# Cosformer attention and a token mixer in one kernel: another order of the same steps, with 16 half products of v on GpSimd and eps of four groups by TensorE

## The chip, the cores and the metric

The kernel runs on one core of a Trainium2 chip. A core has TensorE (matmuls and transposes, which write to PSUM), VectorE (DVE), ScalarE (ACT), GpSimd (POOL) and SyncE (SP), which here issues all DMAs between HBM and SBUF. The metric is the time of one execution on the device in microseconds, as the median of several runs.

## The reference

Attention with a linear kernel over 8 batches, 8 heads, 576 positions and head size 64, then a token mixer over the result. With c = cos and s = sin of pi/2 * position / 576:

```python
def phi(x, c, s):
    r = np.maximum(x, 0.0)
    return np.concatenate([r * c, r * s], axis=-1)
kv = einsum('bhsf,bhsd->bhfd', phi(k), v)
num = einsum('bhsf,bhfd->bhsd', phi(q), kv)
den = einsum('bhsf,bhf->bhs', phi(q), phi(k).sum(axis=2)) + 1e-06
x = (num / den), heads side by side: [8, 576, 512]
W = (x @ w_q) @ (x @ w_k).T / sqrt(64)        # [8, 576, 576]
out = relu(W @ x) @ w_out
```

## The kernel before

The work is cut into 16 groups H of four heads (two pairs of heads), two for each batch b = H // 2. The kernel has one function for each kind of step, and a string, `ORDER` (lines 26 to 67), names every step in the order in which it is issued; the loop at line 555 reads it word by word. Each engine works through its own steps in that order and waits, by semaphores, for what a step needs. So the order of the string is, for each engine, the order of its queue: a step that waits holds all later steps of its engine.

A word is a kind, a number, `a` or `b` where it is half a step (one of the two pairs of heads), `:n` for the PSUM bank where a TensorE step writes (eight banks; most steps take a pair of them, MX, KV, QT, N, XT and XR; WK, WQ, KX and WO take one), and `@A`, `@V`, `@G` for the engine where it can be chosen: ScalarE, VectorE, GpSimd.

- Loads by SP: LK, LQ, LV bring k, q, v of one group in halves of 288 KB into `raw` (line 117), five buffers each, so that a load of group H waits until group H - 5 has been read. LW brings the weights. ST stores a block of 128 output rows from one of 16 `o` buffers.
- RK and RQ (lines 222 and 225) are the relus of k and q to bf16, on any of three engines. The product of v with cos and sin is made in one of two ways: VG (line 239) on GpSimd straight from the loaded v, or CV (line 229), a cast to bf16 on any engine, and then VS (line 232) on VectorE.
- KV (line 268) makes the sums over positions on TensorE, KE (line 304) takes them to SBUF. QT (line 290) transposes q, QM (line 312) multiplies it with cos and sin on VectorE; groups in `QT_WIDE` have another shape of these.
- N (line 332) makes numerator and denominator of half a group, g = 2H or 2H + 1. EP (line 354) adds eps to the denominator; groups in `EPS_PE` have it added by two small matmuls (line 348) instead. RC (line 377) takes the reciprocal of one g, RJ (line 380) of both of a group, X (line 383) multiplies: x in SBUF. RC, RJ and X are VectorE's.
- XT or XR transposes x on TensorE, XE evicts it. WK and WQ are the products of x with w_k and w_q, KW and QW evict them. KX is the product of x with WK's result, [64, 512]; XK evicts it and XA and XB copy halves across partitions. MX makes the mixed rows of a quarter of a batch, ME evicts them with the relu. WO (line 504) multiplies 128 rows with w_out: its rows i count over two batches, nine blocks to each pair; OE evicts, ST stores.
- WU are warm-up matmuls; T steps make tables.

The product with w_k comes first for keys, so the 576 x 576 matrix is never made. v2, rk, rq, vb, qm, kv, x, xT have two buffers each: KV of group H must be through before VG or VS of group H + 2 begins, and so on. In PSUM a step waits until the last reader of its banks is done: `KV0:2` then `N1:2` means that N1 waits for KE0. No step is planned at run time; the string is the whole schedule.

Lines of the profile name the helper: L205 is the relu on VectorE or GpSimd, L203 on ScalarE, L209, L211 and L213 are casts and copies on ScalarE, GpSimd and VectorE, whichever step asked for them; the tile names tell which it was.

Of the kernel before, what the change touches and what calls it, by code (L numbers as in the profile page):

```python
# [43 lines left out]
WO8:1 ME10@V ME11@A RK8a@G LQ11b ME9@A VS9 QT9:6 OE8:5@A LQ10b KV8:4 OE3:6@A LK10b WU4:1 RK9a@G QM9
KE8@A XR7:2 MX8:0 N16:4 VG10a LK11b ME8@A KV9:6 XE7@V EP16@A LK11a RQ11a@A WO10:0 RC16 KE9@A LK12a
X16 WK3:1 LK10a VG10b OE10:7@V N17:4 KW3@A N19:6 LV11b EP17@V N18:0 RC17 EP19@A X17 KX3:2 LQ13b
WQ3:3 EP18@V RJ9 XK3@A LV12b RQ11b@A WO12:4 XA3@G QW3@V LV12a XB3@A VG11a X18 RQ10@A WO11:5 X19
WO2:0 OE12:8@A LQ15b RK11b@A LQ12a QT11:6 OE2:9@V OE11:10@A RK11a@G LK13b XT9:2 RK10b@A LQ14b QM11
XT8:0 XE9@A VG11b LQ14a WO5:5 XE8@V LQ12b RK10a@A QT10:6 MX15:0 MX12:2 QM10 WK4:4 ME12@A CV12@G
# [5 lines left out]
KW5@A ST16 KV13:2 QM13 LV15b VG14b MX16:6 LV15a KE13@A KX5:4 ME16@A LK15a MX17:0 N26:2 XK5@V LK15b
ME17@A N24:6 EP26@V N25:4 RC26 RK14@A X26 WO18:0 XB5@G RQ15@G EP24@V EP25@A RC24 WO20:1 X24
OE18:12@A XA5@G RC25 N27:2 X25 OE20:6@A WQ5:0 ST20 EP27@V RC27 KV14:4 QW5@A X27 VG15 MX20:0 XR12:6
KE14@V ME20@A XR13:2 QT14:4 XE12@A XE13@V WO21:0 QM14 RK15b@A WO15:1 RK15a@A OE21:15@V QT15:4 MX22:6
N28:2 QM15 ME22@A ST21 WK6:0 EP28@A ST11 OE15:6@A KV15:6 ST6 RC28 KW6@A X28 ST4 N29:4 KE15@A MX23:0
ST2 MX21:6 ME23@V KX6:2 ST10 ME21@A ST17 WQ6:3 EP29@A XK6@A RC29 ST1 N30:6 XA6@G QW6@V N31:0 X29  # L60
XB6@G EP30@A ST13 WO22:3 EP31@A ST18 RC30 X30 WO24:2 OE22:10@A ST7 RC31 X31 WO19:3 ST8 ST0 OE24:9@V
MX26:0 OE19:3@A XR15:6 ST9 XR14:4 XE15@V WO26:3 XE14@A ST15 ME26@V ST22 WO23:2 OE26:1@V WK7:4
OE23:13@A ST26 MX27:0 ST12 MX25:6 KW7@V MX24:2 ME27@A WQ7:5 ME24@V ST23 ME25@A KX7:4 ST19 WO28:6
XK7@A ST24 QW7@A XA7@G WO30:7 XB7@G OE28:11@V MX28:4 ST28 MX29:2 ME28@A WO27:6 ME29@V OE30:10@A
MX31:2 MX30:4 OE27:1@V ST30 ME31@A WO25:7 ME30@A ST27 WO29:6 OE25:13@A WO32:4 ST25 OE29:3@V WO31:7
# [5 lines left out]
def kernel(  # L71
# [240 lines left out]
    def QM(H, ps, eng):  # L312
        if H in QT_WIDE:
            q_t = qt_wide(place["QT", H]).rearrange("p c (r d) -> p r c d", r=2)
            for r in range(2):
                V.tensor_mul(  # L316
                    qm_b[H % NQM][:, :, r, 0:C, :],
                    q_t[:, r].unsqueeze(1).to_broadcast([P, 2, C, H2]), qtab)
# [58 lines left out]
    def RC(g, ps, eng):  # L377
        V.reciprocal(rec(g), num(place["N", g])[:, :, :, D:D + 1] if g in EPS_PE else rec(g))  # L378

# [219 lines left out]
```

## Time and profile before

| | before |
|---|---|
| median of 3 runs | 121.09 us (120.91 to 121.33) |
| the profiled execution | 120.56 us, its span 118.8 us |
| granted TensorE clock | 0.998 |
| busy: TensorE, VectorE, ScalarE, GpSimd | 96.0, 90.9, 83.9, 72.1 us |
| moved | 29.62 MB read, 9.44 MB written |

The span runs from the first to the last instruction that the profiler saw. A row of a timeline or of the chain of waits has the start, the length, the engine and line, and the tiles written and read; a row in square brackets tells how long the engine had been idle and what ended it. A row of the groups has the count, the busy time in all and the mean of one in ns. A suffix q means the engine's sequencer, which waits or issues.

### The profile page before, as it was taken

Reading aid. Unit: us, or ns where it says so; the run is one execution under the profiler, and the core shown is the slowest. Engines: PE = TensorE matmul, PEld = TensorE weight load, DVE = VectorE, ACT = ScalarE, POOL = GpSimd, SP = SyncE. Lnnn points to the kernel's source line nnn. Section 1 sums busy time; section 2 is a strip of 40 time slices with the busy share of each in tenths; the row PEclk is TensorE's granted clock in tenths of the full one; section 3 lists DMA queues with packets and bytes.
Section 4 is the critical chain, followed back from the end, with each engine's and each line's share of the span. In section 5 each row is a group of like instructions: output and inputs, shape, how many; then the busy total and the mean of one; then the engine's idle time right before and its main releaser. Section 6 shows DMA issues by size and latency. Waiting matters only on the chain.

```text
span 118.8 us, 4916 instructions
## 1 busy us (share of the span) xinstructions
PE 96.0 (81%) x2068; PEld 66.8 (56%) x2079; DVE 90.9 (76%) x160; ACT 83.9 (71%) x151; POOL 72.1 (61%) x66
## 2 busy tenths in 40 slices
PE   0020797669799789989989989999999999999970
...
DVE  2039699786997998989989787888899988855360
...
GB/s 107 304 370 408 393 388 338 383 390 393 387 393 392 384 389 393 394 389 387 387 391 390 283 348 289 290 345 206 206 279 103 91 302 377 404 393 383 337 299 177
DMA packets 20662, 39.38 MB, mean 332 GB/s; under 512 B 3232, under 2 KB 3232, under 8 KB 20640
## 3 DMA queue, kind: packets, MB, share of 16 engines
...
HBM read 29.62 MB, written 9.44 MB: 329 GB/s over the span
## 4 chain that ended last, share of the span: by engine, by line
PE 48%; DVE 18%; DMA 15%; POOL 5%; issue 5%; ACT 4%; SPq 1%; DVEq 0%; ACTq 0%; POOLq 0%
PE ps L509 19%; DMA vraw<-in_v_dram 10%; DVE qm L316 7%; DVE x L393 5%; DMA kraw<-in_k_dram 5%; PE ps L285 5%; PE ps L340 4%; PE ps L466 4%; PE ps L489 3%; POOL v L248 3%; PE ps L439 3%; PE ps L295 2%; PE ps L452 2%; PE ps L275 2%; PE ps L419 2%
## 5 line engine op out<-in xcount | busy, mean ns | idle before, releaser
L248 POOL TENSOR_TENSOR v<-vraw,vtab 128x1152 bf16<-128x1152 f32 (+1 forms) x16 | 45.1, 2829 | 17.5 <-DVE rec L378 11.4
L509 PE MATMUL ps<-wow,mix 128*128 128x512 bf16 x133 | 33.1, 380 | 0.8 <-issue 0.3
L393 DVE TENSOR_TENSOR x<-ps,rec 128x640 bf16<-128x640 f32 x32 | 25.9, 822 | 1.2
L509 PEld LDWEIGHTS <-mix 128*128 128x128 bf16 x144 | 12.9, 98 | 14.7 <-issue 0.9
L500 ACT ACTIVATE mix<-ps 128x576 bf16<-128x576 f32 x25 | 15.7, 653 | 5.7 <-PE ps L489 5.6
L209 ACT COPY o<-ps 128x512 f32<-128x512 f32 x22 | 12.7, 585 | 9.2 <-PE ps L509 9.0
L316 DVE TENSOR_TENSOR qm<-ps,qtab 128x1152 bf16<-128x1152 bf16 x22 | 15.6, 749 | 0.8 <-PE ps L295 0.8
L211 POOL TENSOR_SCALAR kx<-kx 64x256 bf16<-64x256 bf16 x12 | 6.3, 524 | 14.6 <-ACT kx L209 12.1
L340 PE MATMUL ps<-kvs,qm 64*128 64x65 bf16 x640 | 13.8, 193 | 1.3 <-ACT kvs L209 0.9
L203 ACT ACTIVATE rq<-qraw 128x576 bf16<-128x576 f32 (+1 forms) x15 | 13.1, 880 | 2.1 <-DMA qraw<-in_q_dram 1.9
L340 PEld LDWEIGHTS <-qm 64*128 64x128 bf16 x640 | 12.5, 96 | 3.2 <-issue 2.6
L213 DVE COPY o<-ps 128x512 f32<-128x512 f32 x14 | 9.6, 688 | 5.6 <-PE ps L509 4.7
L203 ACT ACTIVATE rk<-kraw 128x576 bf16<-128x576 f32 (+1 forms) x17 | 12.3, 739 | 0.2
L209 ACT CAST kvs<-ps 128x260 bf16<-128x260 f32 (+1 forms) x14 | 6.6, 471 | 8.1 <-PE ps L275 4.2
L285 PE MATMUL ps<-v,rk 64*64 64x130 bf16 x360 | 7.5, 228 | 5.1 <-DVE v L234 4.0
L209 ACT COPY xT<-ps 128x1152 bf16<-128x1152 bf16 (+1 forms) x8 | 9.3, 1169 | 0.7 <-PE ps L406 0.5
L285 PEld LDWEIGHTS <-rk 64*64 64x64 bf16 x360 | 6.3, 111 | 6.0 <-issue 4.3
L234 DVE TENSOR_TENSOR v<-vb,vtab 128x2304 bf16<-128x2304 bf16 (+1 forms) x8 | 9.1, 1148 | 0.4 <-PE ps L285 0.3
L301 PE MATMUL ps<-ident,rq 64*128 64x64 bf16 x90 | 2.4, 200 | 8.3 <-ACT rq L203 7.3
L489 PE MATMUL ps<-wq,kx 64*128 64x288 bf16 x64 | 8.1, 287 | 0.4 <-DVE x L393 0.4
L275 PE MATMUL ps<-v,rk 64*128 64x260 bf16 x108 | 7.1, 271 | 1.5 <-DVE qm L316 0.9
L295 PE MATMUL ps<-ident,rq 128*128 128x128 bf16 x99 | 7.8, 228 | 0.0
...
## 6 DMA issues: line engine op xcount, KB each, us to landing
...
```

The costliest lines, as they stand in the source:

```text
L203: A.activation(dst, s, AF.Relu)
L209: A.copy(dst, s)
L213: V.tensor_copy(dst, s)
L248: G.tensor_mul(dst[:, part, :, :, 0:D], s[:, part].unsqueeze(3).to_broadcast([P, n, C, 2, D]), vtab.unsqueeze(1).to_broadcast([P, n, C, 2, ...
L285: nc.tensor.matmul(kv_v[o, r, :], rk_of(H)[a, pr, c, :], v2_b[H % NV2][a, pr, c, :, 0:D + 1], start=(c == 0), stop=(c == C - 1))
L295: nc.tensor.transpose(qt_v[:, c, :], rq_b[H % NPREP][:, c, :, :], ident)
L316: V.tensor_mul(qm_b[H % NQM][:, :, r, 0:C, :], q_t[:, r].unsqueeze(1).to_broadcast([P, 2, C, H2]), qtab)
L340: nc.tensor.matmul(nv[:, pr, u, :], qm_b[H % NQM][a, s, r, 2 * u:2 * u + 2, :], kv_b[H % 2][a, r, pr if H in KV_WIDE else 0, s, 0:D + 1], ...
L393: V.tensor_tensor(x_b[b % NX][:, :, 4 * h:4 * h + 4, :].rearrange("p u (w r) d -> p r w u d", r=2)[:, r], nv[:, :, :, 0:D], rec(g).to_broa ...
L489: nc.tensor.matmul(pair(ps)[:, t, :].bitcast(FP32)[:, 0:HS], kx_b[b % 2][a, (m // 2) ^ t, (m % 2) * P:(m % 2 + 1) * P], wq_b[b % 2][a, :], ...
L500: A.activation(dst, s, AF.Relu, scale=scale_moe)
L509: nc.tensor.matmul(o, mix_b[bp % 2][:, m, rt * P:(rt + 1) * P], wow[:, m, :], start=(m == 0), stop=(m == NDM - 1))
```

## The change

`ORDER` is replaced as a whole: 651 words in place of 656. The same functions and buffers are used. Counted over both strings: VG 13 halves and 3 whole groups before, 8 and 4 after (19 and 16 halves); VS 5 whole and 3 halves before, 6 and 4 after. GpSimd takes 5 steps of CV (4 before), 4 of CW (3), 11 of RK (8), 7 of RQ (6), 1 of XB (6). VectorE evicts 8 OE (14), 6 XE (8), 5 KE (2), 8 ME (7); ScalarE 28 OE (22), 10 XE (8), 11 KE (14), 24 ME (25). EP falls from 30 to 28, RC rises from 22 to 24, RJ falls from 5 to 4. Warm-up matmuls are 5 and 1 before, 1 and 2 after. Every TensorE step of the computation is there in both. The engine of a step and its PSUM bank change too. The start and the end of both strings, and the lines around the loads of k for groups 13 and 14:

```diff
@@ ORDER @@
-LV0b TB TQ LQ0b LQ0a TI LV1b TW LK0a LV1a TK LV0a TZ CV0b@A LK0b T2 LV2b LQ1a RQ0@A LQ1b LK1a TV
-QT0:0 RK0a@V LK2b CV1b@V QM0 LK1b CV1a@A LV2a CV0a@A VS1b LQ2a RK0b@A VS0 LQ2b LK2a CV2b@V KV0:0
-VS1a LV3a KE0@A VS2b LV3b RQ1@A N0:0 LW1 N1:2 RK2b@A LQ3b QT1:4 EP1@V RK1a@A RC1 X1 VG2a LQ3a RK1b@A
-WU22:6 QM1 RQ2a@A LW0 KV1:2 LK3a RQ2b@V LK3b RK2a@G KE1@A RC0 QT2:4 X0 LV4b N2:2 KV2:6 QM2 VG3 LQ4a
-N3:0 KE2@A LV4a EP2@V CW1@A N5:6 EP3@A LK4b N4:4 RJ1 EP5@A X2 RQ3@A LQ4b X3 LQ5b XT0:2 CW0@A LQ5a
-EP4@V RK3a@A XT1:0 RC4 X4 LK4a XE0@A RK3b@G QT3:4 LV5b VG4b XE1@A QM3 KV3:2 LV5a LK5a WK0:0 RC5
-KE3@A X5 LK5b N7:2 KW0@A N6:4 RQ4a@G EP7@V RC7 KX0:0 RQ4b@A LV6b X7 VG4a RK4b@A QT4:6 LV6a RC6 X6
-XK0@A XT2:2 RQ5a@A LV7b QM4 WQ0:0 RK4a@A LQ7b XR3:4 RQ5b@G QW0@A KV4:6 LQ7a XE3@A CV5b@V XE2@V
-CV5a@G LQ6b QT5:0 KE4@A XB0@G LK6a WK1:4 VS5 N9:6 LK6b KW1@A MX3:2 RK5b@A N8:4 RK5a@G QM5 LV7a EP9@A
-ME3@A KV5:0 VG6 LQ6a XA0@A EP8@V RJ4 LK7a X9 KX1:2 KE5@A LK7b X8 N10:0 N11:6 RQ7@A LW4 EP10@V XT4:4
-EP11@V RJ5 LW3 X11 WQ1:3 XE4@A LW2 X10 MX2:6 QW1@A MX1:4 LW5 RK6@V XK1@A XR5:0 ME2@A QT7:2 XA1@G
-XE5@V LV8b ME1@A XB1@G KV6:6 CV7@A QM7 RQ6@G LQ8b MX5:4 LQ8a WK2:2 KE6@A VS7 MX0:0 ME5@A LQ9b QT6:6
-KW2@A LK8b MX6:4 RK7b@A KX2:3 QM6 CW3@G LQ9a ME0@A WQ2:2 RK7a@G LV8a ME6@A MX4:0 QW2@V ME4@A CW2@G
-LK8a KV7:6 CW4@V MX7:0 LV9a CW5@G XK2@V KE7@A N13:4 ME7@V XA2@A N14:6 XB2@G LV9b EP13@A N12:2 VG8b
-EP14@A RC13 WO7:0 EP12@V RQ8a@A X13 LK9b RQ8b@A WO1:1 RC12 LQ11a X12 LK9a QT8:4 OE7:0@V OE1:1@A
...
-X23 WO13:2 ST14 RK12@A QM12 RQ13@G WO17:3 LK14a LK14b OE13:13@A XR11:0 XA4@G OE17:14@A XR10:4 RK13@G
...
-ST29 OE32:9@A WO33:6 ST32 OE31:10@V WO35:4 ST31 OE33:1@V WO34:7 ST33 OE35:13@V ST35 OE34:9@A ST34
+LV0a TB TK LQ1a TQ TV LV0b WU6:0 LQ0a LV1a TI LV1b T2 LQ0b TW TZ LK0b LK0a LQ1b CV0@G LV2b LK2b
+CV1a@V LK1a CV1b@V LV2a VS0 RQ0b@A LK1b RK0b@A LQ2b VS1 RK0a@A LQ2a RQ0a@V RQ1@G LK2a QT0:0 LV3b
+KV0:2 QM0 LK3b LV3a QT1:4 KE0@A CV2b@V RK2b@V LQ3b WU10:6 VS2b LW1 N1:2 RK1@G QM1 N0:0 EP1@A LQ3a
+KV1:4 RQ2@A LK3a CV2a@V EP0@V VS2a LV4b RK2a@G QT2:6 RC0 X0 LV4a VG3b QM2 RK3b@A LQ4a KV2:0 KE1@A
+LK4a RC1 N2:4 KE2@A N3:6 RC2 N4:0 X1 VG3a LW0 CW1@A X2 LQ4b XT0:2 RQ3b@A LV5a RC3 N5:4 XE0@A X3 LV5b
+EP4@V RQ3a@G EP5@V XT1:6 RC4 RK3a@A X4 LK4b VG4b QT3:2 XE1@A RC5 LQ5a KV3:0 QM3 LQ5b WK0:6 KE3@V
+LK5b LK5a VG4a X5 N6:0 N7:2 EP6@A LV6a RQ4@A XT2:4 RC6 KW0@V LQ7b X6 EP7@A XE2@A QT4:6 LV6b RC7
+CV5@G X7 KX0:0 LQ6b CW0@A QM4 XR3:2 RK4a@A RK4b@G LK6b WQ0:1 XE3@A KV4:6 LQ6a RQ5@V XK0@A LW4 VS5
+QT5:2 KE4@A WK1:0 LQ7a RK5@A XA0@G QM5 N9:6 N8:4 LW3 KW1@A KV5:2 XB0@A LK6a EP8@A EP9@V RC8 X8 KX1:0
+VG6 LW2 KE5@A QW0@A RC9 N10:2 X9 LQ8a XK1@A N11:4 EP10@A MX3:0 LV7a EP11@V MX2:6 ME3@A RJ5 X10 XB1@A
+LW5 XT4:0 ME2@A X11 LV7b WQ1:2 RQ6@A XE4@V LQ8b MX0:4 XR5:6 RQ7@A QW1@V LQ11b ME0@V MX7:2 CW4@G
+QT6:0 LK7b ME7@A XE5@V QT7:4 XA1@G LK7a RK6@A CW3@G QM6 WK2:6 LV8a CW2@G MX1:0 KW2@A KV6:2 LK8a
+ME1@A QM7 CW5@G LK9b MX5:0 MX6:6 ME5@A WQ2:4 CV7@G LK8b KE6@V KX2:5 QW2@A ME6@V LV8b N13:2 N12:0
+VS7a LV9a MX4:6 WO1:4 ME4@A VS7b LV10b EP13@A EP12@A WO6:6 OE1:0@A RJ6 RK7a@G LQ10b X12 RK7b@A WO4:4
+RQ8@G LV9b OE6:1@A XK2@V X13 KV7:0 LQ9b OE4:2@A XA2@G XB2@A QT8:6 KE7@V LQ9a VG8a XR6:4 QM8 N14:0
...
+ME11@V LK11b RQ9@G MX9:4 KE8@V XR7:0 ME9@A LK10a N17:2 VS9 XE7@A QT9:4 LK13a WO10:6 RK9a@A RQ11a@G
+QM9 WK3:0 OE10:6@A RQ11b@G LK14a KV9:4 LK11a KW3@V VG10 LV12b WQ3:6 RC17 KE9@A X17 CV11a@A LV13a
...
+WO35:1 ST33 OE32:13@V WO34:2 ST32 OE35:8@V ST35 OE34:4@A ST34
@@ sizes @@
-    EPS_PE = (0, 6)
+    EPS_PE = (2, 3, 17, 19)
...
-    QT_WIDE = (1, 4, 5, 6, 7, 8, 9, 10, 11, 12, 14)
+    QT_WIDE = (1, 4, 5, 6, 7, 8, 9, 10, 11, 12, 15)
```

A word such as `WU22:6` means 22 // 4 = 5 warm-up matmuls of shape 2.

More of the change, by code (lines that the diff above doesn't have):

```diff
@@ L44 @@
[L44 to L49, printed above, removed]
@@ L50 @@
-ME15@A KV10:6 OE5:11@V KW4@A KV11:2 KE10@A VS12 ST5 MX13:4 KE11@A N20:6 ME13@A LK12b MX14:0 KX4:2
-LK13a EP20@A VG13a ME14@A WQ4:3 RC20 LV14b X20 XK4@A LV14a N21:0 RQ12a@A N23:4 LQ15a EP21@V QW4@A
-N22:6 RC21 ST3 X21 WO9:2 RQ12b@A VG13b EP23@A EP22@A WO14:3 XB4@A RJ11 OE9:11@A X22 QT12:0 OE14:12@A
-X23 WO13:2 ST14 RK12@A QM12 RQ13@G WO17:3 LK14a LK14b OE13:13@A XR11:0 XA4@G OE17:14@A XR10:4 RK13@G
-XE11@V MX18:6 KV12:2 ME18@A XE10@V RQ14@A MX19:0 VG14a WO16:6 KE12@V ME19@V WK5:7 OE16:6@A QT13:0
@@ L55 @@
[L55 to L65, printed above, removed]
-ST29 OE32:9@A WO33:6 ST32 OE31:10@V WO35:4 ST31 OE33:1@V WO34:7 ST33 OE35:13@V ST35 OE34:9@A ST34
+LV0a TB TK LQ1a TQ TV LV0b WU6:0 LQ0a LV1a TI LV1b T2 LQ0b TW TZ LK0b LK0a LQ1b CV0@G LV2b LK2b
@@ new lines @@
+VS7a LV9a MX4:6 WO1:4 ME4@A VS7b LV10b EP13@A EP12@A WO6:6 OE1:0@A RJ6 RK7a@G LQ10b X12 RK7b@A WO4:4
+RQ8@G LV9b OE6:1@A XK2@V X13 KV7:0 LQ9b OE4:2@A XA2@G XB2@A QT8:6 KE7@V LQ9a VG8a XR6:4 QM8 N14:0
+LK9a XE6@A N15:2 WO7:6 LV11a EP14@V RC14 EP15@A X14 LQ11a WO3:7 VG8b OE7:3@A RK9b@A LK10b MX10:0
+MX8:4 OE3:4@V RK8@A WO8:6 LV10a RC15 X15 WO0:7 LQ10a ME10@A CV9@G ME8@A LV11b MX11:0 KV8:2 OE8:5@A
+ME11@V LK11b RQ9@G MX9:4 KE8@V XR7:0 ME9@A LK10a N17:2 VS9 XE7@A QT9:4 LK13a WO10:6 RK9a@A RQ11a@G
+QM9 WK3:0 OE10:6@A RQ11b@G LK14a KV9:4 LK11a KW3@V VG10 LV12b WQ3:6 RC17 KE9@A X17 CV11a@A LV13a
```

22 lines of the change are left out of this document (20 added, 2 removed).

## The prediction

> **What bounds the kernel now.** I read the page first, then stages of the span, then the chain of waits with the timeline beside it, then the groups of instructions by shape.
>
> ```profile
> span 118.8 us, 4916 instructions
> PE 96.0 (81%) x2068; PEld 66.8 (56%) x2079; DVE 90.9 (76%) x160; ACT 83.9 (71%) x151; POOL 72.1 (61%) x66
> ...
> PE   0020797669799789989989989999999999999970
> ...
> DVE  2039699786997998989989787888899988855360
> ```
>
> TensorE has almost nothing to do for four slices (12 us), is 60 to 90% busy until about slice 16, and is full from there to the end; VectorE is at 80% or more for most of that time. So two things can move the end: how much of TensorE's work is left when it becomes full, and the idle time after that. I cut the span where the opening ends, at the start of KV7, the moment after QM6, the last of the eight QM steps 0 to 7 on VectorE:
>
> ```profile
> 0.00:7.91 7.91, 0.58 (x18) 0.50 (x18) 0.81 (x6) 5.42 (x9) 3.39 (x17) 1.00 0.75 242
> ...
> 0.00:46.35 46.35, 29.68 (x700) 24.15 (x700) 34.09 (x62) 34.37 (x57) 30.02 (x36) 1.00 1.01 362
> 46.35:118.80 72.45, 66.31 (x1370) 42.62 (x1379) 56.78 (x99) 49.50 (x94) 42.08 (x32) 1.00 0.86 312
> ```
>
> The columns are the stage, its length, then busy time of TensorE, its weight loads, VectorE, ScalarE and GpSimd, the granted clock, the DMA share and GB/s. The chain of waits ends on TensorE:
>
> ```profile
> 45.05 0.67 PE ps L466 x10
> 45.72 0.49 PE ps L452 x8
> 46.20 0.23 PE ps L489 x2
> ...
> 108.92 6.16 PE ps L509 x28
> ```
>
> The last product ends at 108.92 + 6.16 = 115.08; the last eviction, store and landing fill the 3.7 us to 118.8. From 46.35 to 115.08 are 68.73 us with 66.31 busy: only 2.42 us of idle TensorE is left to win there. Before 46.35 TensorE was busy 29.68 us, so 16.7 us idle: the opening is where an order can win or lose.
>
> VectorE sets the pace of the opening. From 7.91, its first real work, to 46.35 it worked 34.09 - 0.81 = 33.28 of 38.44 us, idle 5.16. These rows show how it begins and where I cut:
>
> ```profile
> 7.33 0.66 PE L301 MATMUL ps<-ident,rq 64*128 64x64 bf16 x18 [7.33 <-ACT rq L203]
> 7.91 0.46 DVE L205 TENSOR_SCALAR rk<-kraw 128x576 bf16<-128x576 f32 x1 [6.06 <-DMA kraw<-in_k_dram]
> ...
> 8.63 1.41 ACT L209 CAST vb<-vraw 128x576 bf16<-128x576 f32 x2 [0.30 <-DMA vraw<-in_v_dram]
> ...
> 44.93 1.42 DVE L316 TENSOR_TENSOR qm<-ps,qtab 128x1152 bf16<-128x1152 bf16 x2 [0.48 <-PE ps L295]
> ```
>
> The fifth load (LK0a) releases VectorE at 7.91 and the sixth (LV1a) ScalarE at 8.63.
>
> **The change, part by part.** Durations by shape on VectorE, and the two of GpSimd's products:
>
> ```profile
> L248 POOL TENSOR_TENSOR v<-vraw,vtab 128x1152 bf16<-128x1152 f32 x13 | 31.4, 2427 | 14.4 <-DVE rec L378 11.4 <-issue 2.6 <-PE ps L285 0.2
> ...
> L213 DVE COPY o<-ps 128x512 f32<-128x512 f32 x14 | 9.6, 688 | 5.6 <-PE ps L509 4.7 <-PE ps L489 0.4 <-DMA out_dram<-o 0.4
> ...
> L234 DVE TENSOR_TENSOR v<-vb,vtab 128x2304 bf16<-128x2304 bf16 x5 | 6.9, 1385 | 0.3 <-PE ps L285 0.3
> ...
> L502 DVE TENSOR_SCALAR mix<-ps 128x576 bf16<-128x576 f32 x7 | 5.3, 755 | 0.7 <-PE ps L489 0.6
> ...
> L378 DVE RECIPROCAL rec<-rec 128x10 f32<-128x10 f32 x20 | 4.2, 211 | 0.7 <-ACT rec L357 0.5
> ...
> L359 DVE TENSOR_SCALAR rec<-ps 128x10 f32<-128x10 f32 x15 | 2.4, 164 | 3.7 <-PE ps L340 3.6
> ...
> L234 DVE TENSOR_TENSOR v<-vb,vtab 128x1152 bf16<-128x1152 bf16 x3 | 2.3, 754 | 0.1
> ...
> L213 DVE COPY xT<-ps 128x1152 bf16<-128x1152 bf16 x2 | 1.5, 750 | 0.0
> L381 DVE RECIPROCAL rec<-rec 128x20 f32<-128x20 f32 x5 | 1.4, 278 | 1.1 <-ACT rec L357 0.8
> L213 DVE CAST wq<-ps 128x288 bf16<-128x288 f32 x3 | 1.4, 458 | 0.2
> L213 DVE CAST vb<-vraw 128x576 bf16<-128x576 f32 x3 | 1.4, 454 | 0.0
> ...
> L205 DVE TENSOR_SCALAR rk<-kraw 128x576 bf16<-128x576 f32 x2 | 1.1, 555 | 6.1 <-DMA kraw<-in_k_dram 6.1
> ...
> L213 DVE CAST kvs<-ps 128x260 bf16<-128x260 f32 x2 | 0.8, 421 | 0.0
> ...
> L205 DVE TENSOR_SCALAR rk<-kraw 128x1152 bf16<-128x1152 f32 x1 | 0.8, 751 | 0.0
> L205 DVE TENSOR_SCALAR rq<-qraw 128x576 bf16<-128x576 f32 x1 | 0.7, 744 | 0.0
> ...
> L213 DVE CAST wk<-ps 128x320 bf16<-128x320 f32 x1 | 0.5, 492 | 0.4 <-ACT o L209 0.4
> ```
>
> *Three half products fewer on GpSimd.* They save it 3 x 2.43 = 7.3 us, of which it takes some back in casts and relus; VectorE's own v products grow from 5 whole and 3 half to 6 and 4, 1.39 + 0.75 = +2.1 us. VectorE gives up six output evictions for it (6 x 0.69 = 4.1 us, late in the kernel), and its sum over all edits changes by a few tenths. The totals decide nothing here; the place does: what VectorE gains it gains in the opening, and what it loses, late.
>
> *VectorE's list up to the cut.* In the new order the step that ends the opening is QM7 (QM6 stands just before it). Up to there the new list leaves out, against the old list up to QM6: CV5b 0.45, five EP 0.82, RJ1 and RJ4 0.56, RK0a 0.56, RK6 0.75, RQ2b 0.74, VS1 in halves 1.51, VS7 1.39, XE2 0.75: 7.53 us. It has in their place: CV1a and CV2a 0.91, three EP 0.49, RC2, RC3, RC8, RC9 0.84, RK2b 0.56, RQ0a 0.74, RQ5 0.75, VS1 whole 1.39, VS2a 0.75, XE4 0.75, KW0 0.49, QW1 0.46, ME0 0.76, KE3: 9.49 us. KE3 on VectorE with 520 elements has no row: at least the 0.42 of 260 elements, at most the 0.69 of the 512 element copy; I take 0.6, nearer the size it has. Net +1.96: 34.09 + 1.96 = 36.05 us up to QM7.
>
> *Where it starts.* Its first two steps, CV1a and CV1b, need the fifth and the sixth load, so CV1b starts at 8.63 (the queue is full, and any load of 288 KB takes the same turn). From there 36.05 - 0.81 - 0.45 = 34.79 us of work remain: QM7 ends at 43.42 if VectorE never waits.
>
> *What it waits for.* Following the new order by hand: after RQ0a it waits for QT0, 0.7 (the 0.66 above, TensorE just starting); RC2 stands behind N2, which stands behind KV2, whose bank X0 empties late: 0.3; RC8 waits for EP8 on ScalarE, which stands behind RK5, KW1 and XB0: 0.3; hand-overs between engines add some 0.7. That is 2.0. The upper end is the 5.16 us of the old opening: QM7 at 48.6. I take 3.0, nearer the waits I can name: **QM7 ends at 46.4**.
>
> *What TensorE has left then.* At this moment the old kernel had also done KX2, WQ2, MX4, MX5 and MX6, which the new order puts behind QM7; the new one has MX7 already. By the three chain rows that is 0.67 + 0.49 + 3 x 0.23 - 0.23 = 1.62 us more work left. Break-even is thus QM7 at 46.35 - 1.62 = 44.73. At 46.4 the new kernel is 1.7 us behind; the bounds of the waits make it -1.3 to +3.9.
>
> *The rest.* After the cut VectorE has 56.78 us to do in the old kernel, about 1.6 less in the new, and GpSimd its saved products. Of TensorE's 2.42 idle us this can return none or all; I take 0.4, since most of these waits are short ones for a step that ended just before, which less load does not remove.
>
> *Eps of four groups by TensorE.* Groups 2, 3, 17, 19 in place of 0 and 6: two more pairs of small matmuls and two EP fewer (0.16 each on VectorE). I set both at nothing: between -0.3 and +0.2, hidden beside the neighbour engine's work. Warm-up matmuls are six before and three after; five of the six ran while TensorE waited. QT_WIDE swaps group 14 for 15: the same work. Nothing of these reaches the sum.
>
> *Queues.* LK13a and LK14a are issued much earlier, LK14a right behind RK9a, which frees its buffer. SP works in order, so LK11a, LV12, LQ12 stand behind that wait, and KV11 and QT12 wait for those. The old queue has one such stop:
>
> ```profile
> SPq L145 <- ACT rq L203: 3.4, 1, 3.4
> ```
>
> It cost nothing visible, and the new loads behind the stop are needed over 5 us after their turn; I set it at nothing.
>
> *GpSimd against VectorE.* One row speaks against moving v products to VectorE:
>
> ```profile
> 32.68 1.35 DVE L234 TENSOR_TENSOR v<-vb,vtab 128x2304 bf16<-128x2304 bf16 x1
> ...
> 32.71 1.58 POOL L211 TENSOR_SCALAR kx<-kx 64x256 bf16<-64x256 bf16 x1
> ...
> 47.74 0.40 POOL L211 TENSOR_SCALAR kx<-kx 64x256 bf16<-64x256 bf16 x1 [0.79 <-DVE kx L213]
> ```
>
> The same small GpSimd copy takes 0.40 us alone and 1.58 when it begins inside VectorE's product: it is held until that ends. Ten such products stand in the new order, eight in the old, and VS2b and VS2a now run beside RK1 and RK2a on GpSimd. RK1 would end 0.75 us later at most, still ahead of QM1, for which KV1 waits anyway; so nothing in the sum. The Trainium skill has this as a rule (SBUF — State Buffer, Who interferes with whom): a VectorE instruction with two SBUF inputs and a GpSimd instruction that reads SBUF shut each other out for a whole instruction, whoever starts first. The trace agrees with its 1.58; by the rule alone the two held relus would add up to 0.75 us each to the sum.
>
> **The sum.** 1.7 - 0.4 = +1.3 us on the profiled execution, which took 120.56 us (1.76 beside its span): 121.9. That execution is 0.5 below the median of 121.09, so in the median **122.4**.
>
> **The rivals.**
>
> *Break-even (121.1).* VectorE waits only its 2.0 named us (QM7 at 45.4, 0.7 behind) and TensorE's later idle gives back the 0.7. For it: VectorE and GpSimd are lighter late. Against: all hand-overs must go as I followed them.
>
> *Faster (119.8).* The same opening, 0.7 behind, and a lighter late part returns 2.0 of the 2.42 us idle: 121.09 + 0.7 - 2.0. It decides once QM7 ends before 45.4 or TensorE's idle after it is under 1 us. For it: VectorE is over 80% busy after the cut, so it may well be what these waits are for. Against: TensorE is already 96% busy there, 66.31 of 68.73.
>
> *Much slower (124.6).* VectorE's opening waits as long as the old one did, 5.16 us; +3.9, less 0.4. For it: old order and new have the same engines and buffers. Against: the old waits include the wait for its first v products, which the new order fills.
>
> That the change would not do what it says can't be: the order is the text itself.
>
> **How the numbers follow.** A measurement of this kernel tells 0.3% (0.36 us) from no change. Chances: forecast 0.54, with its own range 121.5 to 123.7; break-even 0.12, faster 0.20, much slower 0.14. A little of the forecast and of break-even falls on the other sides: faster 0.22, same 0.12, slower 0.66. The range 119.7 to 124.3 cuts about half of the faster and half of the much slower case: 2 in 10.
>
> **What would show it.** VectorE should be busy about 36 us when QM7 ends, and that end should lie between 45.5 and 47.5; TensorE should then have 1.6 us more work left, and idle about 2 us from there to its last product. The forecast is wrong if QM7 ends before 44.7, or if TensorE's idle after it falls under 1 us; the queue part is wrong if TensorE waits for a relu or product of group 11 or 12 that waited for its load; the lock is worth something if KV1 or KV2 waits for GpSimd's relu.

## The result and the profile after

The kernel after takes 122.62 us in the median of 13 runs (121.77 to 124.12), the kernel before beside it 121.09 us. The ratio is 1.0126, with a 95% interval of 1.0093 to 1.0159: slower by 1.5 us. The profiled execution of after took 122.39 us, that of before 120.56. Executions over 1.5% longer than the fastest of their kernel are left out of the ratios below; the profiled ones of two experiments, opening_of_after and four_local_waits, are of this kind, so of them only single rows are read.

The page of after, first its busy times, then the slices:

```profile
PE 97.2 (81%) x2069; PEld 66.6 (55%) x2080; DVE 91.5 (76%) x163; ACT 82.7 (69%) x146; POOL 68.4 (57%) x63
...
PE   1000976897998889979999899999999899999970
...
DVE  2039699898988999986898986988799879226540
```

In slices 5 to 16, the opening, VectorE has eleven digits of 8 or 9 where it had eight, and late in the kernel it has the lower ones; TensorE is nearly full from about the same slice as before. TensorE is busy 1.2 us longer (97.2 against 96.0).

The windows of after, with the columns of those of before: up to the end of QM7, from there to the last product, and from the start of KV7 to the last product:

```profile
0.00:45.60 45.60, 28.38 (x679) 23.38 (x680) 35.80 (x65) 28.61 (x47) 29.68 (x36) 1.00 1.00 358
45.60:116.95 71.35, 68.86 (x1395) 43.17 (x1400) 55.67 (x99) 53.46 (x98) 38.76 (x28) 1.00 0.87 312
50.51:116.95 66.44, 64.00 (x1319) 40.48 (x1328) 51.03 (x91) 49.83 (x91) 36.23 (x25) 1.00 0.86 307
```

QM7 ends at 45.60 with 35.80 us of VectorE's work done. From there TensorE has 68.86 us to do (66.31 before) and idles 71.35 - 68.86 = 2.49 us (2.42 before). The last product ends at 116.95, 1.87 us later than before.

Both kernels can also be cut at the start of KV7, 46.36 before and 50.51 after. TensorE idles 2.44 us from there in the new order, 2.42 in the old. These are TensorE's groups by line in these two windows, first of before (46.35 to 115.08), then of after (50.51 to 116.95); a row has the count, the busy time and the mean of one, then the idle time ahead of them:

```profile
L509 PE MATMUL ps<-wow,mix 128*128 128x512 bf16 x133 | 33.1, 380 | 0.8 <-issue 0.3
L340 PE MATMUL ps<-kvs,qm 64*128 64x65 bf16 x400 | 8.1, 190 | 0.3 <-DVE qm L316 0.3
L489 PE MATMUL ps<-wq,kx 64*128 64x288 bf16 x52 | 6.4, 287 | 0.1
L285 PE MATMUL ps<-v,rk 64*64 64x130 bf16 x324 | 6.3, 219 | 1.1 <-DVE qm L316 0.9 <-DVE x L393 0.2
...
L419 PE MATMUL ps<-ident,x 64*128 64x64 bf16 x160 | 3.3, 190 | 0.1
...
L548 PE MATMUL ps<-warm 64*64 64x384 bf16 x1 | 0.3, 321 | 0.0
```

```profile
L509 PE MATMUL ps<-wow,mix 128*128 128x512 bf16 x123 | 30.9, 380 | 1.1 <-DVE qm L316 0.6
L340 PE MATMUL ps<-kvs,qm 64*128 64x65 bf16 x360 | 7.4, 190 | 0.4 <-DVE qm L316 0.4
L285 PE MATMUL ps<-v,rk 64*64 64x130 bf16 x324 | 6.7, 220 | 0.2
L489 PE MATMUL ps<-wq,kx 64*128 64x288 bf16 x48 | 6.2, 287 | 0.0
...
L419 PE MATMUL ps<-ident,x 64*128 64x64 bf16 x160 | 3.7, 190 | 0.3 <-DVE qm L316 0.3
...
L348 PE MATMUL ps<-epsr,ones 64*128 64x5 bf16 x4 | 0.4, 165 | 0.0
```

KV7 starts 50.51 - 46.36 = 4.15 us later, but more stands ahead of it: three WO (12 matmuls), two N (40) and one MX (2). By the differences of these rows that is 2.2 + 0.7 + 0.2 us, and 0.3 for a warm-up that the new order no longer has behind KV7: 3.4 us. The rows count too little of WO and too much of MX, for some records of WO are missing (133 of 144) and the window of before begins inside an MX; by the timeline of after at this place, shown below, two N take 0.8 us and three WO 2.7 up to KV7, 3.7 us with the MX. So 0.4 to 0.7 us are lost up to KV7. After KV7 the idle time is equal, and what is left is dearer: a row of 0.4 for eps, and the same 324 KV and 160 XR matmuls are busy 0.4 us longer each kind, at the same mean of one. I read this as less overlap with what stands around them. By the rows of the groups 0.7 + 0.4 + 0.8 = 1.9, the 1.87 of the end. Rows of lines overlap a little, so this account is good to some 0.3 us, and it tells where the time stands, not what causes it.

What it waits for shows in the chain of waits. Its shares of the span by engine, first of before, then of after:

```profile
PE 48%; DVE 18%; DMA 15%; POOL 5%; issue 5%; ACT 4%; SPq 1%; DVEq 0%; ACTq 0%; POOLq 0%
```

```profile
PE 49%; DVE 30%; issue 7%; ACT 5%; DMA 4%; SPq 2%; DVEq 0%; ACTq 0%
```

VectorE's share of the chain has grown from 18 to 30%, though it is busy only 0.6 us longer over the whole. Some links of after's chain late in the kernel:

```profile
60.20 1.43 DVE qm L316 x2
61.67 0.72 PE ps L285 x36
...
66.84 1.34 DVE qm L316 x2
68.22 0.72 PE ps L406 x10
...
95.00 1.43 DVE qm L316 x2
96.48 0.48 PE ps L340 x20
```

At 61.67, 68.22 and 96.48 TensorE begins a step as soon as a pair of QM products on VectorE has emptied its banks (the second is XT9, the third N29). After 96.48 the chain stays on TensorE to the last product.

### The profile page after: what moved, and what is told of

Read it like the earlier page. It is cut to its first block, busy times and chain, and to the rows that moved or that the text cites. A ratio compares the mean times of both kernels' runs of the same rounds, so it can differ in the third digit from the quotient of the medians.

```text
span 120.6 us, 4906 instructions
## 1 busy us (share of the span) xinstructions
PE 97.2 (81%) x2069; PEld 66.6 (55%) x2080; DVE 91.5 (76%) x163; ACT 82.7 (69%) x146; POOL 68.4 (57%) x63
## 4 chain that ended last, share of the span: by engine, by line
PE 49%; DVE 30%; issue 7%; ACT 5%; DMA 4%; SPq 2%; DVEq 0%; ACTq 0%
PE ps L509 22%; DVE qm L316 9%; DVE x L393 7%; PE ps L285 5%; DVE v L234 5%; DMA vraw<-in_v_dram 4%; PE ps L489 4%; PE ps L340 4%; PE ps L466 3%; PE ps L275 2%; PE ps L452 2%; PE ps L295 2%; SPq L145 2%; PE ps L439 2%; ACT rk L203 2%
## 5 line engine op out<-in xcount | busy, mean ns | idle before, releaser
L248 POOL TENSOR_TENSOR v<-vraw,vtab 128x1152 bf16<-128x1152 f32 (+1 forms) x12 | 37.2, 3107 | 7.1 <-DMA vraw<-in_v_dram 2.4
L209 ACT COPY o<-ps 128x512 f32<-128x512 f32 x28 | 16.1, 585 | 7.7 <-PE ps L509 7.6
L203 ACT ACTIVATE rq<-qraw 128x576 bf16<-128x576 f32 (+1 forms) x12 | 11.0, 923 | 4.7 <-DMA qraw<-in_q_dram 4.5
L205 POOL TENSOR_SCALAR rk<-kraw 128x576 bf16<-128x576 f32 (+1 forms) x11 | 9.6, 876 | 7.4 <-DMA kraw<-in_k_dram 5.0
L209 ACT COPY xT<-ps 128x1280 bf16<-128x1280 bf16 (+1 forms) x10 | 11.8, 1180 | 1.3 <-PE ps L419 1.3
L211 POOL TENSOR_SCALAR kx<-kx 64x256 bf16<-64x256 bf16 x7 | 3.7, 522 | 14.8 <-DVE kx L213 8.6
L234 DVE TENSOR_TENSOR v<-vb,vtab 128x2304 bf16<-128x2304 bf16 (+1 forms) x10 | 11.8, 1194 | 0.0
L203 ACT ACTIVATE rk<-kraw 128x576 bf16<-128x576 f32 (+1 forms) x13 | 10.2, 794 | 1.2 <-DMA kraw<-in_k_dram 1.1
L205 POOL TENSOR_SCALAR rq<-qraw 128x1152 bf16<-128x1152 f32 (+1 forms) x7 | 7.2, 1040 | 6.6 <-DMA qraw<-in_q_dram 4.4
L502 DVE TENSOR_SCALAR mix<-ps 128x576 bf16<-128x576 f32 x8 | 6.0, 754 | 3.7 <-PE ps L489 2.9
```

The source lines that it names most:

```text
L203: A.activation(dst, s, AF.Relu)
L205: eng.tensor_scalar(dst, s, FMAX, 0.0, op0=ALU.min, op1=ALU.max)
L209: A.copy(dst, s)
L234: V.tensor_mul(v2_b[H % NV2][:, part, :, :, 0:D], vb_b[H % NPREP][:, part].unsqueeze(3).to_broadcast([P, n, C, 2, D]), vtab.unsqueeze(1).t ...
L248: G.tensor_mul(dst[:, part, :, :, 0:D], s[:, part].unsqueeze(3).to_broadcast([P, n, C, 2, D]), vtab.unsqueeze(1).to_broadcast([P, n, C, 2, ...
```

## The experiments

Two theories stood against each other. The theory of the opening is that of the prediction: VectorE's longer list makes the start late, and the rest only carries that to the end. The theory of the rest: the opening costs little, and the new order after it loses the time in its own waits. The times of steps below are the starts of their first weight loads in the profiled execution; the first matmul follows within 0.1 us, for WO34 0.2 us later and for KV10 in the order of before 0.5. The loads land up to 0.6 us earlier or later from one execution to the next, so a kernel with the same opening is read by how its distance to after changes from KV7 to WO34, the last WO. Each ratio is to the executions of before made beside that kernel, with medians of 120.94 to 121.19 us.

| kernel | median us | ratio to before, 95% | KV7 | KV10 | KV15 | WO34 |
|---|---|---|---|---|---|---|
| before | 121.09 | | 46.36 | 70.72 | 94.42 | 113.83 |
| after | 122.62 | 1.0126 [1.0093, 1.0159] | 50.51 | 69.53 | 96.89 | 115.69 |
| opening_of_before | 122.68 | 1.0108 [1.0066, 1.0150] | 50.41 | 69.36 | 96.86 | 115.66 |
| opening_of_after | 123.56 | 1.0161 [1.0114, 1.0207] | 48.31 | | | |
| before_opening_on_vector | 123.20 | 1.0184 [1.0135, 1.0232] | 48.46 | 72.69 | 96.39 | 116.54 |
| eps_two_groups | 122.63 | 1.0121 [1.0075, 1.0166] | 50.26 | 69.52 | 96.89 | 115.69 |
| dose_opening | 122.89 | 1.0119 [1.0069, 1.0168] | 50.22 | 69.24 | 96.61 | 115.40 |
| dose_x19 | 122.64 | 1.0152 [1.0124, 1.0179] | 50.38 | 69.75 | 97.13 | 115.92 |
| evictions_58_68 | 122.04 | 1.0109 [1.0069, 1.0150] | 50.26 | 69.07 | 96.75 | 115.54 |
| qt15_before_wo21 | 122.03 | 1.0095 [1.0062, 1.0128] | 49.91 | 68.92 | 96.07 | 114.87 |
| three_local_waits | 122.03 | 1.0094 [1.0064, 1.0125] | 49.88 | 68.69 | 96.41 | 115.21 |
| four_local_waits | 123.08 | 1.0135 [1.007, 1.020] | | | | |
| v11_on_gpsimd | 126.10 | 1.0399 [1.0349, 1.0448] | 50.46 | 71.91 | 100.88 | 119.68 |
| v11_behind_rk10 | 123.62 | 1.0221 [1.0176, 1.0266] | 50.87 | 69.88 | 98.18 | 116.98 |

### The two openings and the two rests, crossed

opening_of_before has the old order up to the place where KV7 stood, and all that is left in the new order (with its QT_WIDE, and a few PSUM banks chosen anew):

```diff
@@ ORDER of before @@
 KW2@A LK8b MX6:4 RK7b@A KX2:3 QM6 CW3@G LQ9a ME0@A WQ2:2 RK7a@G LV8a ME6@A MX4:0 QW2@V ME4@A CW2@G
-LK8a KV7:6 CW4@V MX7:0 LV9a CW5@G XK2@V KE7@A N13:4 ME7@V XA2@A N14:6 XB2@G LV9b EP13@A N12:2 VG8b
+LK8a LQ11b MX7:6 CW4@G ME7@A CW5@G LK9b N13:4 N12:0 LV9a WO1:2 LV10b EP13@A EP12@A WO6:6 OE1:0@A RJ6
...
-    EPS_PE = (0, 6)
+    EPS_PE = (0, 6, 17, 19)
```

> The order of before up to KV7, then what is left in the order of after (four PSUM banks chosen anew; eps by TensorE for groups 0, 6, 17, 19). Theory A, the opening sets it: VectorE works to the end of QM7 as in before, so nearly the whole 1.5 us comes back: 120.9 to 121.4 us. Theory B, the rest of the new order costs it (eps matmuls and waits where TensorE is full): 122.2 to 122.7 us. Both halves by the two profiles (1.1 from the opening, 0.7 from the rest): 121.5 to 121.9 us.

122.68 us: the old opening brings nothing back. This is TensorE's timeline at the seam, of opening_of_before and then of after:

```profile
46.64 0.49 PE L340 MATMUL ps<-kvs,qm 64*128 64x65 bf16 x20
47.30 0.48 PE L340 MATMUL ps<-kvs,qm 64*128 64x65 bf16 x20 [0.17 <-ACT mix L500]
47.71 2.76 PE L509 MATMUL ps<-wow,mix 128*128 128x512 bf16 x11
50.41 0.72 PE L285 MATMUL ps<-v,rk 64*64 64x130 bf16 x36
```

```profile
46.97 0.79 PE L340 MATMUL ps<-kvs,qm 64*128 64x65 bf16 x40
...
47.82 2.76 PE L509 MATMUL ps<-wow,mix 128*128 128x512 bf16 x11
50.52 0.72 PE L285 MATMUL ps<-v,rk 64*64 64x130 bf16 x36
```

At its first N the old opening is 0.3 us ahead; its second N then waits for a mixed row that ScalarE evicts, and at WO1 and KV7 only 0.1 us is left of its lead. It entered this seam on time (KV6 at 41.63, 41.51 in before) and still ends like after: with the new rest the old opening is worth nothing.

opening_of_after is the reverse: the new order up to KE6 on VectorE, then what is left in the old order (with its QT_WIDE), with eps on TensorE for groups 2 and 3:

```diff
@@ ORDER of after @@
-ME1@A QM7 CW5@G LK9b MX5:0 MX6:6 ME5@A WQ2:4 CV7@G LK8b KE6@V KX2:5 QW2@A ME6@V LV8b N13:2 N12:0
+ME1@A QM7 CW5@G LK9b MX5:0 MX6:6 ME5@A WQ2:4 CV7@G LK8b KE6@V LV8b VS7 LQ9b RK7b@A KX2:3 LQ9a RK7a@G
...
-    EPS_PE = (2, 3, 17, 19)
+    EPS_PE = (2, 3)
```

> The order of after up to CV7 and KE6, then what is left in the order of before (eps by TensorE for groups 2 and 3 alone). Theory A, the opening sets it: 122.3 to 122.7 us. Theory B, the rest sets it: 120.9 to 121.3 us. Both: 121.9 to 122.3 us.

123.56 us, the slower of the two crossings in their medians. KV7 starts 1.95 us later than in before, after a wait of 0.82 us for a mixed row of ScalarE: the old rest has KV7 at once and nothing to do meanwhile. Up to here this execution is level with after (QM7 ends at 45.63 and 45.60), so these rows can be read; of the 1.95 us, 0.82 are a wait that neither whole order has. So the new opening is late for the old rest and hardly for the new one. Neither half alone is the cost; each half is slower with the other order than before is as a whole.

### Does VectorE set the pace?

before_opening_on_vector gives four evictions of the old opening to VectorE, with no other edit:

```diff
@@ ORDER of before @@
-KE3@A X5 LK5b N7:2 KW0@A N6:4
+KE3@V X5 LK5b N7:2 KW0@V N6:4
...
-EP11@V RJ5 LW3 X11 WQ1:3 XE4@A LW2 X10 MX2:6 QW1@A
+EP11@V RJ5 LW3 X11 WQ1:3 XE4@V LW2 X10 MX2:6 QW1@V
```

> Before, with four evictions of its opening (KE3, KW0, XE4, QW1) by VectorE in place of ScalarE, as the new order has them: 2.3 us more VectorE ahead of QM6. Theory A, VectorE's load sets the pace of the opening: KV7 starts 1 to 2 us later and the end follows, 122 to 123 us. Theory F, the opening has as much slack on VectorE as its idle time (5.2 us) and is set by loads and hand-overs: KV7 within 0.4 us of before, the end within 0.5 us.

Its windows, cut at the start of KV7 (the second ends where its last product does, to 0.2 us):

```profile
0.00:48.45 48.45, 30.90 (x700) 24.52 (x700) 36.64 (x66) 32.12 (x53) 29.50 (x36) 1.00 1.01 362
48.45:118.00 69.55, 67.47 (x1381) 42.65 (x1379) 56.32 (x99) 48.82 (x94) 41.48 (x30) 1.00 0.86 305
```

VectorE is busy 36.64 us up to KV7 where it was 34.09, and KV7 is 2.1 us late; at KV10 it is still 2.0, and WO34 is 2.7 us late. So in the old order VectorE's work in the opening passes almost in full to the end, as the prediction had it.

dose_opening and dose_x19 add one memset on VectorE to after, behind X3 in the opening or behind X19 in the middle. I meant it to last 0.75 us; it was issued as 384 words in place of 768 elements and took half:

```diff
+    dum = pool.tile([P, 768], BF16, name="dum")
+    def DD(i, ps, eng):
+        V.memset(dum, 0.0)
...
-XE0@A X3 LV5b
+XE0@A X3 DD LV5b
...
-X19 RK11b@A
+X19 DD RK11b@A
```

> After, with one more VectorE instruction in the opening, a memset of 128 x 768 bf16 (some 0.75 us) behind X3. Theory A (VectorE is the pace of the opening): the end comes later by nearly all of it, 0.6 to 0.8 us. Theory B (loads or other engines set the opening, VectorE has slack there): under 0.3 us.

> After, with the same small VectorE memset as in the run with a dose in the opening (0.38 us there, and absorbed before QM5), now behind X19. Theory C (VectorE paces here): KV10 starts 0.3 to 0.4 us later than in after, and the end 0.1 to 0.4 us. Theory D: KV10 unchanged within 0.1 us.

VectorE's timeline in dose_x19:

```profile
64.09 0.82 DVE L393 TENSOR_TENSOR x<-ps,rec 128x640 bf16<-128x640 f32 x1
64.95 0.38 DVE L539 MEMSET dum<- 128x384 uint32 x1
```

In dose_x19 KV7 stands 0.13 us ahead of after, KV10 0.22 behind, WO34 0.23 behind: the 0.38 us come out as 0.36 at the end. The late order has no slack at this place. In dose_opening X3 is 0.39 ahead of after's and KV7 0.29 ahead, so 0.10 of the 0.38 has passed by this pair. But kernels with the same opening and no dose differ among themselves in this stretch: from X3 to KV7 after takes 27.09 us, dose_x19, evictions_58_68, qt15_before_wo21 and three_local_waits 26.89, eps_two_groups 27.18; with the dose it is 27.19. So between nothing and 0.3 us of the dose passes, and this run does not settle it. From KV7 on its distance to after is unchanged (0.29 at WO34). With medians of 122.9 and 122.6 the times alone show nothing of so small a dose.

### Eps on TensorE

```diff
-    EPS_PE = (2, 3, 17, 19)
+    EPS_PE = (2, 3)
...
-RC17 KE9@A
+EP17@V RC17 KE9@A
...
-N18:4 N19:0 OE0:7@A
+N18:4 N19:0 EP19@A OE0:7@A
```

> After, with eps of groups 17 and 19 by VectorE and ScalarE as in before, and of 2 and 3 by TensorE as in after. The matmuls of eps take 0.4 us of TensorE after the opening, where it is full: if they lie on its path the time falls by 0.2 to 0.4 us, to 122.2 to 122.4; as predicted (hidden) it stays within 0.2 us of 122.6.

122.63 us. KV7 stands 0.25 us ahead of after, KV10 and WO34 level with it. So in these two executions eps of groups 17 and 19 by the other engines costs 0.25 us, too little for the medians to tell. From KV7 to the last product TensorE is busy as long without the four matmuls as with them:

```profile
50.26:116.95 66.69, 64.01 (x1315) 40.53 (x1324) 51.47 (x92) 50.02 (x92) 36.28 (x25) 1.00 0.86 306
```

64.01 against 64.00, and it idles 0.24 us more, while VectorE has 0.4 us more to do (51.47 against 51.03). The row of 0.4 us for eps in the account above is thus not what the change pays: TensorE is the cheaper place.

### Mending single waits

Each of these mends something on which TensorE waits in after. evictions_58_68 takes three evictions from VectorE between 58 and 68 us; qt15_before_wo21 puts the last wide transposes ahead of a WO, so that QM15 starts earlier; three_local_waits has both, and RQ14 later, behind OE20, for whose bank KV14 waits; four_local_waits also CV13a earlier.

```diff
@@ evictions_58_68 @@
-ME11@V LK11b RQ9@G MX9:4 KE8@V
+ME11@V LK11b RQ9@G MX9:4 KE8@A
...
-KV9:4 LK11a KW3@V
+KV9:4 LK11a KW3@A
...
-EP18@V QW3@V
+EP18@V QW3@A
@@ qt15_before_wo21 @@
-XE12@V OE15:12@A MX22:0 WO21:3 RQ15b@A ST15 XE13@V ME22@A ST7 QT15:4 OE21:15@A
+XE12@V RQ15b@A OE15:12@A MX22:0 QT15:4 WO21:3 ST15 XE13@V ME22@A ST7 OE21:15@A
@@ three_local_waits: both, and @@
-X25 XB5@A RQ14@A EP26@V
+X25 XB5@A EP26@V
...
-X24 OE20:11@A
+X24 OE20:11@A RQ14@A
@@ four_local_waits: these, and @@
-KE11@V N20:4
+KE11@V CV13a@V N20:4
...
-WO9:4 XA4@G CV13a@V
+WO9:4 XA4@G
```

> After, with KE8, KW3 and QW3 by ScalarE as most of their kind (1.5 us of VectorE less between 58 and 64 us). Theory C, VectorE paces the stretch from VS9 to QM11 (it is 5.9 of 6 us busy from 64 to 70): QM11 ends 0.4 to 0.7 us earlier, KV10 starts so much earlier, and the end moves by 0.2 to 0.6 us. Theory D, the rest is paced by TensorE and its banks: KV10 and the end stay within 0.15 us in the profile.

122.04 us. Against after it is 0.25 us ahead at KV7, 0.46 at KV10, and 0.15 at KV12 and WO34. The 0.2 us won up to KV10 are gone at KV12, and the loss has a place: CV13a on VectorE, 0.76 us in after, takes 1.37 (rows of the same place follow below).

> After, with two words moved: QT15 ahead of WO21 on TensorE and RQ15b ahead of OE15 on ScalarE. QM15 then comes some 0.5 us earlier and WO21 fills the time in which N29 waited for it. If that wait (0.7 us at N29) is lost time, the end is 0.3 to 0.6 us earlier; if something else is late next, under 0.15 us.

122.03 us. 0.60 us ahead of after at KV7, 0.82 at KV15 and at WO34: the mend is worth 0.2 us, and these stay.

> After, with four of its local waits in the rest mended at once: KE8, KW3, QW3 by ScalarE; CV13a on VectorE ahead of EP21, in a gap where GpSimd stands still; RQ14 behind OE20 on ScalarE (KV14 waits for OE20's bank); QT15 ahead of WO21 and RQ15b ahead of OE15. If the 1.5 us are lost in such waits, in the rest: the gains add up along the order, 0.2 at KV10, 0.5 to 0.7 at KV12, 0.8 to 1.0 at KV14, 0.9 to 1.3 at the end: 121.3 to 121.7 us. If each is taken up by what is late next: under 0.5 us.

123.08 us, with the widest interval of all. In the profiled execution KV7 is 0.5 us behind after and KV12 2.1, and these rows of its timeline stand between:

```profile
73.99 2.38 POOL L248 TENSOR_TENSOR v<-vraw,vtab 128x1152 bf16<-128x1152 f32 x1 [0.90 <-PE ps L489]
74.14 2.54 DVE L213 CAST vb<-vraw 128x576 bf16<-128x576 f32 x1
```

CV13a, moved ahead to a free place, began 0.15 us after a product of GpSimd and ended 0.3 us after it: 2.54 us for a cast that takes 0.45 alone.

> As the kernel with four mends, but CV13a stays where the new order has it: the three evictions KE8, KW3, QW3 on ScalarE, RQ14 behind OE20's predecessor XB5, QT15 and RQ15b ahead of WO21. If the failure of the four mends was CV13a, which in its new place ran into GpSimd's VG12a, then this kernel should lie at 121.7 to 122.2 us, with VectorE's CV13a at 1.4 us or less, KV15 at 96.3 to 96.7 (96.89 in the kernel after) and WO34 at 114.7 to 115.3 (115.69). If the mends don't add up anyhow, because what each gives is taken up by the next wait, it is 122.4 to 122.9 and WO34 starts at 115.5 or later, with CV13a short.

The place behind XB5, which this text gives for RQ14, is the one that it has in after; the edit above moves it behind OE20.

122.03 us, in the band of the theory that CV13a was what went wrong. But by its own start little is won: 0.63 us ahead of after at KV7, 0.84 at KV10, 0.51 at KV12 and 0.48 at WO34. QM15's wait is gone, and CV13a in its old place runs into GpSimd as in evictions_58_68. The timeline of three_local_waits:

```profile
76.80 1.15 POOL L205 TENSOR_SCALAR rq<-qraw 128x1152 bf16<-128x1152 f32 x1
76.87 1.38 DVE L213 CAST vb<-vraw 128x576 bf16<-128x576 f32 x1
```

The 0.2 us of the QT15 mend are missing too: from KV14 to KV15 three_local_waits takes 6.76 us, after 6.73 and qt15_before_wo21 6.53. RQ14 is what differs. Behind OE20 it holds back QW5 on ScalarE, whose bank QT14 needs, and TensorE waits there, as it does not in after (after's row first, then that of three_local_waits):

```profile
91.11 0.44 PE L301 MATMUL ps<-ident,rq 64*128 64x64 bf16 x18
```

```profile
90.84 0.44 PE L301 MATMUL ps<-ident,rq 64*128 64x64 bf16 x18 [0.47 <-ACT wq L209]
```

So the mends don't add up in the trace: the 0.2 us of the evictions are paid back at the next meeting of VectorE and GpSimd, and the third mend opens a wait of its own. None of these kernels is told from after by its time (all intervals overlap with that of after), and none reaches before.

### The product of group 11 back to GpSimd

GpSimd is busy only 68.4 us in after, so two kernels give it group 11's product straight from the load (VG11, two halves) in place of CV11a, CV11b and VS11, one ahead of RK10 in GpSimd's queue and one behind it:

```diff
@@ v11_on_gpsimd @@
-KE9@A X17 CV11a@A LV13a
+KE9@A X17 LV13a
...
-ST12 CV11b@G XT8:4 LV13b OE11:9@A LV15b RK10@G XT9:0
+ST12 VG11 XT8:4 LV13b OE11:9@A LV15b RK10@G XT9:0
...
-KV10:4 VS11 XK3@A
+KV10:4 XK3@A
@@ v11_behind_rk10: the same, but for @@
-ST12 VG11 XT8:4 LV13b OE11:9@A LV15b RK10@G XT9:0
+ST12 XT8:4 LV13b OE11:9@A LV15b RK10@G VG11 XT9:0
```

> After, with v of group 11 made by GpSimd as in before (one whole product: 18 halves in place of 16; CV11 and VS11 are left out, VectorE 1.35 us less at 69 us, ScalarE 0.7, GpSimd some 3.9 more). The three halves moved to VectorE as a cost: the end is 0.4 to 1.0 us earlier. As the profile reads (QM10 behind VS11 waits 0.5 us for QT10 anyway, GpSimd has 4 us idle before VG12): within 0.3 us of after.

126.10 us, a miss: I had not counted what is queued behind VG11. GpSimd's timeline:

```profile
61.44 9.09 POOL L248 TENSOR_TENSOR v<-vraw,vtab 128x2304 bf16<-128x2304 f32 x2
70.50 1.35 POOL L205 TENSOR_SCALAR rk<-kraw 128x1152 bf16<-128x1152 f32 x1
```

RK10 starts at 70.50, KV10 waits 2.4 us for it, and the delay grows from 2.4 us there to 4.0 at WO34. The granted clock accounts for the growth. This is the window from 72 to 76 us, right behind that wait, and the last three figures are the granted clock, the DMA share and GB/s:

```profile
72.00:76.00 4.00, 3.78 (x64) 2.79 (x66) 1.42 (x2) 0.96 (x2) 3.23 (x2) 0.58 0.98 361
```

It is 0.58 there and 0.99 to 1.00 in the windows around it; 4 us at 0.58 lose 4 x 0.42 = 1.7 us, the growth from 2.4 to 4.0. Five of the six executions of this kernel have a mean clock of 0.980 to 0.984 and took 125.75 us or more, the sixth 1.000 and 124.71.

> As the run with v of group 11 on GpSimd, but with the product behind RK10 in GpSimd's queue and not ahead of it. If the 4 us there were RK10 waiting in the queue, KV10 is back at its place and the end is within 0.4 us of after (122.2 to 123.0); if GpSimd as a whole is too full for 18 halves, the end stays 2 us or more above after.

123.62 us, with a granted clock of 1.00 in the profiled execution. Now KV10 is in time (0.35 us behind after, as at KV7), and the next victim is VectorE:

```profile
67.50 4.57 POOL L248 TENSOR_TENSOR v<-vraw,vtab 128x2304 bf16<-128x2304 f32 x1
...
69.10 3.29 DVE L205 TENSOR_SCALAR rk<-kraw 128x576 bf16<-128x576 f32 x1
...
72.30 1.41 DVE L316 TENSOR_TENSOR qm<-ps,qtab 128x1152 bf16<-128x1152 bf16 x2
...
73.99 0.42 PE L285 MATMUL ps<-v,rk 64*64 64x130 bf16 x14
```

RK11a on VectorE takes 3.29 us in place of 0.45: it ends 0.3 us after GpSimd's product does (72.07). QM10 stands behind it, and KV11 waits for QM10's bank and starts at 73.99, 1.3 us later than in after. So GpSimd's idle time is not free here: its product held a relu of VectorE until it was done.

The Trainium skill (SBUF — State Buffer, Who interferes with whom) has the rule for this: besides instructions with two SBUF inputs, casts and scalar operations of VectorE in its two-port modes lock against GpSimd for a whole instruction, and whoever is second waits. The 3.29 and 2.54 us here agree: both end some 0.3 us after GpSimd's product.

## Why the prediction was right, and where it was not

The forecast was +1.3 us, the result is +1.5: the side is right, and the time lies within the stated range. That the size came so near is in part luck, for two terms of the sum were off in opposite ways: the lag of the opening was smaller than forecast and all but gone at KV7 when the same list follows, and the rest, which was to give back 0.4 us, loses more than a microsecond.

*VectorE's list up to the cut*: 36.05 us forecast, 35.80 measured. *Where it starts*: CV1b at 8.63, measured 8.51. *What it waits for*: 3.0 us; 45.60 - 8.51 less 34.5 us of work leaves 2.6. **QM7 ends at 46.4** came out as 45.60. Up to here the steps held, each with 0.1 to 0.4 us to the good side.

*What TensorE has left then* went wrong in two ways. By busy time it had 2.55 us more left, not 1.62 (68.86 against 66.31); but by the account by lines 1.2 of that is the dearer part after KV7, not more steps. And the size of the lag, 1.7 us behind at the cut (0.87 by the measured 45.60 and the same break-even), did not last: opening_of_before, which is on time at the cut, is only 0.3 ahead at the first N and 0.1 at KV7. What I left out is that the seam of the new order has its own wait, for a mixed row of ScalarE, which the late kernel no longer meets. The mechanism is real where the order is fixed (before_opening_on_vector: 2.5 us more on VectorE, KV7 2.1 us late), and in front of the old rest the new opening is late by 1.95 us (opening_of_after, 0.82 of it a wait of that seam); but the lag against another list of steps has to be taken behind the seam, with the new list ahead of it.

*The rest* has the wrong sign. I let it give back 0.4 us of TensorE's idle 2.42, for VectorE and GpSimd are lighter there. They are (55.67 us on VectorE after the cut, 56.78 before), and the idle time stayed at 2.49. Instead the rest loses some 1.7 us, and opening_of_before shows that it does so with the old opening too. By the account by lines 0.4 to 0.7 of the 1.87 us stand ahead of KV7 and 1.2 to 1.4 behind it. An estimate from the starts of TensorE's steps, by the work left (each step at the time that it takes in these traces when nothing holds it), has after 0.8 us behind before at the cut, 0.4 at KV7, 0.5 to 1.1 from 52 to 80 us (1.4 for a moment at 70), 1.2 to 1.4 from 82 to 92 and 1.8 from 98 on. Why a lighter VectorE gives nothing is argued, not shown: in dose_x19 a QM on VectorE holds TensorE's banks directly, and 0.38 us in front of it come out as 0.36, while the three evictions less of evictions_58_68 win 0.2 us and lose it again. Single waits are worth 0.2 us each (qt15_before_wo21), or nothing once the next one takes them up (evictions_58_68, three_local_waits). So it is a loss in many small places and I found none that carries it. Why the same KV and XR matmuls are 0.8 us longer busy is read as less overlap at more breaks; no run shows it by itself.

*Eps of four groups* was set at nothing, between -0.3 and +0.2: the two later groups gain 0.25 us in the profiled execution (eps_two_groups). No run tests the warm-up matmuls or QT_WIDE by themselves.

*Queues.* LK14a does hold SP as I described, for its relu:

```profile
SPq L145 <- ACT rk L203: 2.5, 1, 2.5
```

2.5 us in place of the old stop's 3.4, and KV11 and QT12 wait for no load: nothing, as forecast.

*GpSimd against VectorE* in the opening. The timeline of after around KV1 and KV2:

```profile
15.38 1.76 POOL L205 TENSOR_SCALAR rk<-kraw 128x1152 bf16<-128x1152 f32 x1 [2.69 <-DMA kraw<-in_k_dram]
...
17.19 0.09 PEld L275 LDWEIGHTS <-rk 64*128 64x128 bf16 x1 [0.49 <-POOL rk L205]
17.52 1.19 PE L275 MATMUL ps<-v,rk 64*128 64x260 bf16 x18 [0.69 <-DVE qm L316]
17.66 0.70 POOL L205 TENSOR_SCALAR rk<-kraw 128x576 bf16<-128x576 f32 x1 [0.52 <-DMA kraw<-in_k_dram]
17.87 1.10 DVE L234 TENSOR_TENSOR v<-vb,vtab 128x1152 bf16<-128x1152 bf16 x1
...
19.13 0.82 DVE L393 TENSOR_TENSOR x<-ps,rec 128x640 bf16<-128x640 f32 x1
...
20.00 1.19 PE L275 MATMUL ps<-v,rk 64*128 64x260 bf16 x18 [1.03 <-DVE x L393]
```

RK1 is held by VS2b and takes 1.76 us; KV1's weights wait for it, but its matmuls wait longer, for QM1's bank. So the lock costs nothing at KV1, as forecast. At KV2 it is the other way round, which I had not weighed: RK2a began first, and VS2a on VectorE takes 1.10 us in place of 0.75. X0 stands behind VS2a, and KV2 waits 1.03 us for X0's bank, so up to 0.35 us of the lock stand in the opening; how much of it reaches the end no run shows. In the rest, too, an instruction of VectorE can be the one that is held (CV13a, RK11a). It is one of the ways in which gains of the rest are taken up.

Of the rivals, break-even and faster needed the rest to give back 0.7 and 2.0 us. It gave back none. Much slower needed 5.16 us of waits in the opening; there were 2.6.
